# Five reorderings in a gated attention kernel: where a projection's products stand, when row factors are spread, which PSUM banks are used at the end, how wide a mask is, and which load goes first

## The chip, the core and the metric

The kernel runs on one core of a Trainium2 chip. The metric is the device time of the whole program in microseconds (us), as the median of repeated runs. One further run was taken with the hardware profiler. Its page and its trace are what is read below. TensorE is written PE in the profile, its weight loads PEld, VectorE is DVE, ScalarE is ACT, GpSimd is POOL, and SyncE, which issues nearly all transfers, is SP.

## The reference

Two attention blocks A and B of 32 heads with 16 channels run on the same x (2048 rows, 512 columns), and a gate mixes them. A is causal attention inside four chunks of 512 rows, mixed with a linear-attention memory that is carried from chunk to chunk. B is full attention over all 2048 rows.

```
g = sigmoid((x * gate_w).sum(-1))
A, for each of 4 chunks of 512 rows:
    p     = softmax(q k^T / 4 + causal mask);  a_dot = p v
    a_mem = (phi(q) M) / (phi(q) z + 1e-6)           # memory of the earlier chunks
    o     = sig(beta) * a_mem + (1 - sig(beta)) * a_dot
    M += phi(k)^T v ;  z += sum(phi(k))
B:  p = softmax(q k^T / 4) over all 2048 rows ;  o = p v
out = g * (oA @ woA) + (1 - g) * (oB @ woB)
```

## The kernel before, in words

The order of every engine's work is written out by hand: an instruction stands in its engine's queue where the Python code calls it, and engines wait for each other only through semaphores that follow from the data.

**First stage (about 0 to 353 us).** x is loaded in 16 tiles of 128 rows (`load_x`), turned on PE (`do_x`), and split into a high and a low part. Queries, keys and values of A and B are projected (`qk_job`, `v_job`: twelve products of 512 columns each, for high and low parts) and stored to DRAM. `dot_gate` on DVE multiplies x with `gw`, which `load_gate` has spread over the partitions. For A, blocks `blk` 0 to 15 stand for four head groups g by four chunks c. In block 1, 5, 9 and 13 `mem_upd(g, 0)` makes the first memory out of turned keys and the values that `load_vm(g, 0)` brought. SP issues in its own order: at the last value tile it loads B's first keys (`load_kb(0)`) and queries (`load_q(32)`), and only at block 0 the memory's values (`load_vm(0, 0)`).

**Pairs (about 353 to 1975 us).** A loop over k from 0 to 31 works on one unit of B and one of A at a time; a unit is four heads by 512 queries. I call one turn of it a pair. It has 37 groups n: 32 for B (two for each of 16 key tiles) and 5 for A. A group is:

- `t_group` (L502): keys times queries into two PSUM banks, then two exponentials on ACT (L508, 128x512 each), and for A a causal select on POOL (L511);
- one task that finds row maxima for the unit after it: `s_b` (L448, two products into a two-bank tile `SBK`, and a DVE reduction of 1024 columns, L450), or `s_a` for A (L427, with the causal mask added by small products, L430, reduced in L434 and L436);
- `pv` (L524): probabilities times values into the bank `PVB`, one key tile behind. Group 1 of a pair has no `pv`.

`m_chain` (four short DVE instructions, L459 to L469, after group 21) and `m_rows` (PE L475, ACT L477, four transfers L483, at group 24) turn the maxima into rows that are appended to the queries. Exponentials of B and A take their banks from a rotation of three, `T3` (TB0, TB1, MB), the one used longest ago first.

**Factors and projection.** Each unit's result goes to DRAM and back (`fin_copy`, `fin_load`); `fin_rec` makes a row factor on DVE; `fin_bc` (SP, L560) spreads it into the tile `d`; `fin_norm` on POOL multiplies (L564), and for later chunks adds (L569), every second pair. POOL takes its work in order but does not wait for the pair's groups, so a `fin_norm` starts when its factor has landed. From pair 8 on, every even pair ends with `out_split` (ACT L583, POOL L584), and `out_mm` does the twelve products of one half of the output projection in each pair from 9 on (L590), before group 20's `pv`; the first half's sum is copied by ACT (L594), the second's added by DVE (L597).

**Last pair and end.** In pair 31 no maxima are left to find, so the two banks of `SBK[0]` join the rotation: five banks. After it the last four row tiles are projected (`tail_mm`, L617) into the four banks of `SBK[1]` and `SBK[0]`, `TAIL`, and copied out in halves by DVE (L628) and ACT (L626).

The mask of `s_a` is two products a block and row half, both 128 columns wide: the first covers query rows 0 to 63 of the block, the second rows 64 to 127. In the second the first 65 columns of the mask are zero, since those keys are not ahead of any such query.

Of the kernel before, what the change touches and what calls it, by code (L numbers as in the profile page):

```python
# [26 lines left out]
EARLY = 6  # L27
S_FIRST = 10
S_LAST = 10
OMI = 10  # L30


@with_exitstack
def gated_mix_kernel(ctx, tc, x, wq, wk, wv, wo, beta, wqkv, wob, gate_w, out):
    nc = tc.nc
# [381 lines left out]
    def s_a(u, i, p):  # L417
        mx = pair_max(chain_of(u))
        n = 128 * (i + 1)
        b = rot("s", SBK)  # L420
        todo_p = [(0, p)] if p is not None else [(0, 0), (256, 1)]
        for c0, p in todo_p:
            for n2 in range(3):
                for j in (1, 0):
                    r = slice(64 * j, 64 * j + 64)
                    if n2 == 0:
                        nc.tensor.matmul(b[:, j, c0:c0 + n], q_of(u)[r, p, i * 128:(i + 1) * 128], k_of(u, p)[r, :n],  # L427
                                         start=True, stop=False)
                    else:
                        nc.tensor.matmul(b[:, j, c0 + n - 128:c0 + n], crows[r, n2 - 1], cmask[r, n2 - 1],  # L430
                                         start=False, stop=n2 == 2)
        m = mx[:, 0].rearrange("q (j p) i -> q j p i", j=2)
        if len(todo_p) == 1:
            nc.vector.tensor_reduce(m[:, :, p, i], b[:, :, :n], axis=AX.X, op=OP.max)  # L434
        else:
            nc.vector.tensor_reduce(m[:, :, :, i], b.rearrange("q j (p k) -> q j p k", p=2)[:, :, :, :n], axis=AX.X,  # L436
                                    op=OP.max)
# [204 lines left out]
        load_x(tt)  # L642
    identity()
    load_w("B", 0)
    load_gate()
    for tt in range(4, 8):
        load_x(tt)
    constants()

    for tt in range(3):  # L650
# [34 lines left out]
    for tt in range(NT):  # L685
        v_job("A", tt)
        if tt == 2:
            split_w(0, "A", 0)
            do_gate()
        if tt == 3:  # L690
            load_beta()
        if tt in (7, 9, 11):
            load_wv("B", (tt - 7) // 2)
        if tt == NT - 1:
            load_kb(0)
            load_q(32)
        if ax:
            set_aux(*ax.pop(0))
# [21 lines left out]
    for blk in range(16):  # L720
        g, c = divmod(blk, 4)
        pg, pc = divmod(blk - 1, 4)
        if blk == 4:
            mode["misc"] = TB + [MB, PVB]
        if 4 <= blk < 14:
            quota += len(ST_A + ST_B) / 10
        if blk == 14:
            for p in range(2):
                set_aux(KB[1][:, p], 0, nc.sync)
            load_kb(1, 0)  # L730
        if blk == 0:
            load_vm(0, 0)
        n = blk + 1 + (c == 2)
        if c < 3 and n < 16:
            load_vm(n // 4, n % 4)
        qk_job(0, "A", g, 0, c)
        if c == 3 and g < 3:
            split_w(0, "A", g + 1, (0,))
        spill()
        if blk == 0:  # L740
            split_wv(3)
            do_beta()
        if blk > 0:
            if pc == 0:
                mem_upd(pg, pc)
        qk_job(0, "A", g, 1, c)
        spill()
        if c == 2 and g < 3:
            load_w("A", g + 1)
        if c == 3 and g < 3:  # L750
            split_w(0, "A", g + 1, (1,))
        if blk == 4:
            load_q(33)
            load_ka(0)
            load_q(0)
            load_va(0)
        if blk == 6:
            load_w("B", 1)
        for f, n in ((store_gate, 5), (load_grow, 7), (do_grow, 10)):
            if blk == n:  # L760
                f()
        if blk == 14:
            m_chain(0)
        if blk == 15:
            m_rows(0)
        want = CUM[blk]
        mt = [[], [], []]
        if c > 0:
            mt[0] += [todo(mem_out, g, c)]
            mt[2] += [todo(mem_put, g, c)]  # L770
        if c < NC4 - 1:
            mt[1 + (c == 0)] += [todo(mem_tr, g, c)]
        for n in range(3):
            for f in mt[n]:
                f()
            if blk == 14 and n == 2:
                quota = EARLY
            if mt[n]:
                spill()
            if blk == 14:  # L780
                load_kb(1, 1 + n)
            if nf == 35:
                mode["misc"] = [MB, PVB, TB[1]]
            if nf < want:
                fill[nf]()
                spill()
                if nf in (18, 24):
                    load_w("B", 2 + nf // 24)
                if nf in (15, 20, 26):
                    split_w(2 if nf == 20 else 1, "B", nf // 5 - 2)  # L790
                nf += 1
        if blk == 13:
            for f in first:
                f()
            first, quota = [], 0
        if 0 < c < NC4 - 1:
            mem_upd(g, c)
        if blk == 14:
            spill()
        if blk == 15:  # L800
            for f in early:
                f()
        if nf >= 16 and "vb" not in AT:
            AT["vb"] = 1
            load_vb(0)
# [13 lines left out]
            set_aux(KB[2][:, p], 0)  # L819

    T3 = TB + [MB]
    TAIL = [b[:, n] for b in SBK[::-1] for n in range(2)]
    mode["misc"] = T3
    NG = 2 * NT + 5

# [22 lines left out]
    def extras(k):  # L848

        pre, post = {}, {}  # L850
        if not k:
            for n in range(4):
                pre[2 * n] = [fill[n - 4]]
        post[2 * S_LAST + 4] = [todo(m_rows, k + 1)]
        for n, it in [(k - 9, OMI)] + [(23, 14)] * (k == 31):
            if n >= 0:
                pre[2 * it] = [todo(out_mm, n // 8, n // 2 % 4, n % 2)]
        return pre, post

    def beside(k, it):  # L860

        for f, it0, u in ((fin_load, NT + 1, 32 + k), (fin_rec, 5, 31 + k), (fin_bc, 6, 31 + k),
                          (fin_load, 1, k - 1), (fin_rec, 6, k - 1), (fin_bc, 7, k - 1)):
            if it == it0 and (k or it0 > NT):
                f(u)
        c, j = divmod(k - 1, 8)
        if k and j % 2:
            for kd, it0 in (("B", 9), ("A", 13)):
                if it == it0:
                    fin_norm(kd, j // 2, c)  # L870
        if k >= 8 and k % 2 == 0 and it == NT + 2:
            out_split(k // 8 - 1, k // 2 % 4)
        if (k, it) == (31, 4):
            grest = AT["grest"] = AT["o"][0][64:, 0, 0]
            nc.sync.dma_start(grest, GD[3 * C:].rearrange("(o t) -> o t", o=1).to_broadcast([64, C]))
        if (k, it) == (31, 9):
            grest = AT["grest"]
            nc.vector.tensor_scalar(grest, grest, nh[64:, 3:4], None, op0=OP.mult)
        if (k, it) == (31, NT + 2):
            fin_rec(63)  # L880
        if k == 31 and it == 13:
            o = AT["o"][1][:64, 3, 0]
            nc.gpsimd.tensor_tensor(o, o, AT["d"][0][:64], op=OP.mult)
        if k == 31 and it < 8 and it % 2 == 0:
            for a in range(2):
                tail_split(it // 2, slice(0, 3), a)
# [17 lines left out]

    for k in range(32):
        ua, ub = k, 32 + k
        banks = T3 + [SBK[0][:, n] for n in range(2)] * (k == 31)
        for n in range(NG):
            it = n // 2 if n < NG - 1 else NT + 2
            t_group(*(ub, n) if n < 2 * NT else (ua, n - 2 * NT), banks)  # L910
            for f in plan.get((k, n), []) + ex[k][0].get(n, []):
                f()
            pvs(k, n)
            for f in ex[k][1].get(n, []):
                f()
            if n % 2 == 0 and n < NG - 1:
                continue
            beside(k, it)
            if it == S_LAST:
                m_chain(k + 1)  # L920
            if it == 4 and not k:
                late()
            if it == 4 and not k:
                load_q(ub + 2)
                for c in range(NC4):
                    load_kb(2, c)
            if it == NT and k < 29:
                load_q(ub + 3)
                load_kb(k + 3)
            if it == 6 and k < 31:  # L930
                load_q(ua + 1)
                load_ka(ua + 1)
                if (ua + 1) % 2 == 0:
                    load_va(ua + 1)
            if it == 9:
                if k % 2 == 0 and k < 30:
                    load_vb(k // 2 + 1)
                if 1 <= k <= 4:
                    load_wo(k - 1)
# [55 lines left out]
```

## Time and profile before

| | |
|---|---|
| median of the runs shown | 2007.81 us (2006.12 to 2014.9) |
| the profiled execution | 2007.75 us; its span 2006.0 us, 1.75 us around it |
| busy: PE, DVE, ACT, POOL | 1956.3, 1631.9, 1435.1, 256.6 us |
| chain that ended last | PE 89%, DMA 3%, DVE 3%, ACT 2%, SP's queue 2% |
| pairs 0 to 31 | start at 352.6 us; pair 9 starts at 801.7, pair 31 at 1924.7, the end begins at 1974.8 |

All times on the trace's axis count from the span's start. A row of the timeline gives start, length, engine, line, operation, tiles (out<-in) and count of merged instructions; in brackets stands the idle time of the engine before it and what ended that. A row of the stretches gives its length, each engine's busy time with its count, and PEclk, the share of full clock that PE was granted. PE's ends are modelled, so starts are the better clock.

### The profile page before, as it was taken

How to read it: one execution, taken by the hardware profiler on the slowest of the kernel's cores; microseconds unless marked ns; L12 is line 12 of the kernel's file. 1: busy time of each engine (PE TensorE's matmuls, PEld its weight loads, DVE VectorE, ACT ScalarE, POOL GpSimd, SP SyncE). 2: the span in 40 equal slices, each digit the busy share in tenths (PEclk: the TensorE clock that was granted, in tenths of full speed). 3: DMA queues.
4: the chain of work that ended last, by engine and by line, in shares of the span. 5: the costliest groups of instructions: out<-in, count | busy, mean ns of one | idle time of the engine just before them, and what ended most of it. 6: DMA issues, size and time to landing. Idle time of an engine off the chain costs nothing.

```text
span 2006.0 us, 43688 instructions
## 1 busy us (share of the span) xinstructions
PE 1956.3 (98%) x17517; PEld 949.0 (47%) x17517; DVE 1631.9 (81%) x1825; ACT 1435.1 (72%) x2703; POOL 256.6 (13%) x474
## 2 busy tenths in 40 slices
PE   8999999999999999999999999999999999999988
PEld 7777777444444344444444444444444444444434
DVE  6135665799999999999999999999899999899832
ACT  3233332688888888888787888787878787878883
POOL 2200000011110101111111111111111111111111
PEclk9999999999999999999999999999999999999999
DMA  7765656644443445343435344444444545444101
GB/s 222 164 190 177 197 180 177 148 106 112 95 112 85 104 93 109 81 110 81 109 79 112 85 112 85 112 85 112 85 112 85 112 85 111 85 112 85 50 26 54
DMA packets 162743, 222.49 MB, mean 111 GB/s; under 512 B 39261, under 2 KB 89453, under 8 KB 156781
## 3 DMA queue, kind: packets, MB, share of 16 engines
q1 hardware_dynamic: 159596, 211.70, 43.9%
q0 software_dynamic: 2944, 8.00, 2.2%
q8 instruction: 138, 2.26, 0.5%
q14 instruction: 65, 0.52, 0.1%
HBM read 148.21 MB, written 68.16 MB: 108 GB/s over the span
## 4 chain that ended last, share of the span: by engine, by line
PE 89%; DMA 3%; DVE 3%; ACT 2%; SPq 2%; issue 1%; POOL 0%; ACTq 0%; POOLq 0%; DVEq 0%
PE pvb L524 31%; PE tb L502 17%; PE sbk L448 12%; PE mb L502 8%; PE tb L279 3%; PE sbk L427 2%; PE tb L590 2%; PE mb L279 2%; ACT raw L508 2%; PE pvb L279 2%; DVE mxb L450 2%; PE sbk L430 2%; PE mb L590 1%; PE sbk L279 1%; PE tb L262 1%
## 5 line engine op out<-in xcount | busy, mean ns | idle before, releaser
L450 DVE TENSOR_REDUCE mxb<-sbk 128x2 f32<-128x1024 f32 x1024 | 1222.7, 1222 | 49.4 <-PE sbk L448 45.7
L508 ACT ACTIVATE raw<-tb 128x512 f32<-128x512 f32 x1557 | 886.0, 596 | 172.8 <-PE tb L502 85.6
L524 PE MATMUL pvb<-raw,vb 128*17 128x256 f32 (+1 forms) x8072 | 639.5, 389 | 0.0
L508 ACT ACTIVATE raw<-mb 128x512 f32<-128x512 f32 x780 | 465.2, 596 | 81.6 <-PE tb L502 57.5
L502 PE MATMUL tb<-qb,xh 64*128 64x512 f32 x880 | 330.9, 494 | 3.7 <-ACT raw L508 3.7
L524 PEld LDWEIGHTS pvb<-raw,vb 128*17 128x17 f32 x8072 | 133.8, 95 | 344.8 <-issue 338.4
L448 PE MATMUL sbk<-xh,qb 64*128 64x512 f32 x1344 | 287.6, 400 | 4.4 <-DVE mxb L450 3.3
L511 POOL TENSOR_SCALAR_AFFINE_SELECT raw<-raw 128x256 f32<-128x256 f32 (+1 forms) x320 | 115.4, 361 | 879.9 <-ACT raw L508 871.9
L502 PE MATMUL mb<-qb,xh 64*128 64x512 f32 x437 | 215.6, 493 | 2.0 <-ACT raw L508 2.0
L502 PEld LDWEIGHTS tb<-qb,xh 64*128 64x128 f32 x880 | 124.7, 183 | 190.5 <-issue 98.3
L502 PE MATMUL tb<-qb,kb 64*128 64x512 f32 x463 | 176.0, 496 | 4.8 <-ACT raw L508 2.8
L434 DVE TENSOR_REDUCE mx<-sbk 128x2 f32<-128x768 f32 (+1 forms) x128 | 139.8, 1092 | 43.9 <-PE sbk L430 36.2
L448 PE MATMUL sbk<-kb,qb 64*128 64x512 f32 x704 | 152.9, 408 | 0.8 <-DVE mxb L450 0.7
L448 PEld LDWEIGHTS sbk<-xh,qb 64*128 64x128 f32 x1344 | 138.8, 186 | 10.8 <-DVE mxb L450 7.0
L502 PEld LDWEIGHTS mb<-qb,xh 64*128 64x128 f32 x437 | 79.9, 183 | 89.5 <-issue 49.1
L502 PE MATMUL mb<-qb,kb 64*128 64x512 f32 x241 | 118.4, 491 | 0.8 <-DVE st L289 0.8
L502 PEld LDWEIGHTS tb<-qb,kb 64*128 64x128 f32 x463 | 65.8, 183 | 102.3 <-issue 51.4
L524 PE MATMUL pvb<-raw,va 128*17 128x256 f32 (+2 forms) x1280 | 94.7, 383 | 4.2 <-ACT pvs L533 0.8
L564 POOL TENSOR_TENSOR o<-o,d 128x512 f32<-128x512 f32 x31 | 39.7, 1282 | 415.2 <-DMA qa<-dA 177.0
L427 PE MATMUL sbk<-ka,qa 64*128 64x256 f32 (+3 forms) x512 | 86.6, 346 | 0.0
L502 PE MATMUL tb<-qa,ka 64*128 64x384 f32 (+3 forms) x340 | 79.5, 372 | 0.0
L448 PEld LDWEIGHTS sbk<-kb,qb 64*128 64x128 f32 x704 | 72.1, 185 | 12.6 <-issue 6.5
(265 smaller groups left out, 1804.5 us busy)
## 6 DMA issues: line engine op xcount, KB each, us to landing
xh<-dB SPq DMA_DIRECT2D x38, 512.0 KB
vb<-vdB SPq DMA_DIRECT2D x16, 1088.0 KB
dB<-st SPq DMA_DIRECT2D x64, 256.0 KB
dA<-st SPq DMA_DIRECT2D x64, 256.0 KB
pd<-pvs SPq DMA_DIRECT2D x64, 256.0 KB
kb<-dB SPq DMA_DIRECT2D x22, 512.0 KB
xh<-dB SPq DMA_DIRECT2D x38, 256.0 KB
qb<-dB SPq DMA_DIRECT2D x64, 128.0 KB
```

What stands on the lines that cost most here:

```text
L279: nc.tensor.matmul(b, WS[ws][w][wi][:, k, :], (XH, XL)[xi][c][:, k, :], start=n == 0, stop=n == 11)
L427: nc.tensor.matmul(b[:, j, c0:c0 + n], q_of(u)[r, p, i * 128:(i + 1) * 128], k_of(u, p)[r, :n], start=True, stop=False)
L430: nc.tensor.matmul(b[:, j, c0 + n - 128:c0 + n], crows[r, n2 - 1], cmask[r, n2 - 1], start=False, stop=n2 == 2)
L434: nc.vector.tensor_reduce(m[:, :, p, i], b[:, :, :n], axis=AX.X, op=OP.max)
L448: nc.tensor.matmul(b[:, j], q_of(u)[r, p, i * 128:(i + 1) * 128], k_of(u, p)[r, kc * C:(kc + 1) * C], start=True, stop=True)
L450: nc.vector.tensor_reduce(MXB[u][:, :, p, i, kc], b, axis=AX.X, op=OP.max)
L502: nc.tensor.matmul(bs[j][:, c0:c0 + w], k_of(u, h // 2)[r, 128 * it:128 * it + 128], q_of(u)[r, h // 2, q0:], start=True, stop=True)
L508: nc.scalar.activation(pt, bs[j], AF.Exp, scale=SCALE)
L511: nc.gpsimd.affine_select(out=m, in_=m, pattern=[[1, 128]] if n < 2 else [[0, 2], [1, 128]], compare_op=OP.is_ge, fill=0.0, base=0, channe ...
L524: nc.tensor.matmul(PVB[32 * h:32 * h + E + 1, q0 + lo:q0 + hi], vt[:, it, 4 * q + h, :], pt[:, lo:hi], start=it == 0 and lo == 0, stop=it ...
L564: nc.gpsimd.tensor_tensor(o, o, d, op=OP.mult)
L590: nc.tensor.matmul(b, (AT["oh"], AT["ol"])[oi][:, g, a], (AT["wh"], AT["wl"])[wi][:, g, a], start=n == 0, stop=n == 11)
```

## The change

- `extras`: the twelve products of `out_mm` move from group 20 (`OMI` = 10, two groups an iteration) to group 1 of each pair from 9 on. `OMI` = 14 now places only the one extra half in pair 31, at group 28, where it was.
- `beside`: `fin_bc` for A's unit k-1 moves from iteration 7 to iteration 12 (`S_LAST` + 2), so in SP's queue it passes the loads of iteration 9 (`vb`, and `om` into `d`), and the transfers of `m_rows`.
- In pair 31 the rotation takes the first bank of each `SBK` tile in place of both banks of `SBK[0]`; `TAIL` becomes TB0, TB1, MB and the first bank of `SBK[0]`.
- `s_a`: the second mask product covers the last 64 columns in place of 128.
- `load_vm(0, 0)` moves from block 0 to the last value tile, ahead of `load_kb(0)` and `load_q(32)`.
- `load_gate` moves behind x's tiles 4 to 7.

```diff
-OMI = 10
+OMI = 14
...
-                        nc.tensor.matmul(b[:, j, c0 + n - 128:c0 + n], crows[r, n2 - 1], cmask[r, n2 - 1],
+                        w = 192 - 64 * n2
+                        nc.tensor.matmul(b[:, j, c0 + n - w:c0 + n], crows[r, n2 - 1], cmask[r, n2 - 1, 128 - w:],
                                          start=False, stop=n2 == 2)
...
     load_w("B", 0)
-    load_gate()
     for tt in range(4, 8):
         load_x(tt)
+    load_gate()
...
         if tt == NT - 1:
+            load_vm(0, 0)
             load_kb(0)
             load_q(32)
...
-        if blk == 0:
-            load_vm(0, 0)
...
-    TAIL = [b[:, n] for b in SBK[::-1] for n in range(2)]
+    TAIL = T3 + [SBK[0][:, 0]]
...
-        for n, it in [(k - 9, OMI)] + [(23, 14)] * (k == 31):
+        for n, at in [(k - 9, 1)] + [(23, 2 * OMI)] * (k == 31):
             if n >= 0:
-                pre[2 * it] = [todo(out_mm, n // 8, n // 2 % 4, n % 2)]
+                pre[at] = [todo(out_mm, n // 8, n // 2 % 4, n % 2)]
...
-                          (fin_load, 1, k - 1), (fin_rec, 6, k - 1), (fin_bc, 7, k - 1)):
+                          (fin_load, 1, k - 1), (fin_rec, 6, k - 1), (fin_bc, S_LAST + 2, k - 1)):
...
-        banks = T3 + [SBK[0][:, n] for n in range(2)] * (k == 31)
+        banks = T3 + [b[:, 0] for b in SBK] * (k == 31)
```

## The prediction

> **What bounds the kernel now.** I read the chain of waits first (PE 89%, in the table above), then the span in 40 slices, then stretches cut at each pair's first exponential, then the timeline where stretches differ.
>
> ```profile
> PE   8999999999999999999999999999999999999988
> ...
> 609.00:657.00 48.00, 47.61 (x500) 19.31 (x494) 45.95 (x48) 40.67 (x77) 3.61 (x10) 1.00 0.41 91
> 657.00:705.70 48.70, 47.60 (x500) 19.15 (x494) 46.74 (x48) 40.72 (x76) 6.17 (x12) 1.00 0.47 103
> 801.70:852.60 50.90, 50.51 (x510) 21.47 (x508) 45.93 (x48) 41.26 (x77) 5.93 (x11) 1.00 0.38 82
> 1669.30:1721.90 52.60, 50.88 (x512) 21.52 (x508) 48.13 (x49) 41.59 (x78) 7.59 (x14) 1.00 0.52 109
> 1924.70:1974.80 50.10, 41.14 (x280) 14.97 (x276) 11.27 (x28) 38.34 (x75) 5.72 (x9) 0.97 0.09 30
> ...
> 801.70:1875.30 1073.60, 1062.43 (x10591) 450.76 (x10588) 975.43 (x998) 869.96 (x1617) 140.28 (x251) 1.00 0.44 95
> ```
>
> The first row is PE's busy share by slice. In the others the length and the busy time of PE, PEld, DVE, ACT and POOL stand behind the stretch; they are pairs 5, 6, 9, 26 and 31, then pairs 9 to 29 together. The reader is to see three things. PE fills a pair (47.61 of 48.00 us), so what PE no longer does or waits for comes off the time; DVE is close behind with 45.95. A pair with twelve products is 2.90 us longer (50.90 against 48.00). Some pairs with the same PE work are longer still (pair 6 by 0.70, pair 26 by 1.70), with DVE busier by 0.8 and 2.2. Pair 31 is another case: no engine is full.
>
> **The change, part by part.** *The memory's values ahead of the keys.*
>
> ```profile
> 104.09 2.15 PE L350 MATMUL sbk<-vm,pk 128*128 128x136 f32 x8 [3.34 <-DMA vm<-vdA]
> ...
> 105.88 3.78 PE L279 MATMUL sbk<-xh,ws 128*128 128x512 f32 x8
> ...
> 104.00:110.70 6.70, 6.61 (x21) 5.68 (x22) 0.30 (x1) 0.00 (x0) 0.00 (x0) 0.55 0.77 258
> ...
> 165.45 1.19 PE L350 MATMUL mb<-vm,pk 128*128 128x136 f32 x8
> ...
> 166.39 2.12 PE L279 MATMUL pvb<-xh,ws 128*128 128x512 f32 x8
> ```
>
> PE stands 3.34 us until the values land, and then runs at a granted clock of 0.55: the eight memory products take 2.15 where they later take 1.19, the next eight 3.78 where others take 2.12. With the load ahead of eight key and query transfers, wait and slow clock both go: 3.34 + 0.96 + 1.66 = 6.0 us. PE is full in the slices that follow (nines above), so they stay gone. Late next are keys and queries, which the first maxima need in block 4 only. Range: 3.3 (the clock drops anyway) to 6.3.
>
> *The projection's products.* Now at group 20, for 2.90 us. The place where they go, then the place where they stand (pair 9):
>
> ```profile
> 801.66 2.37 POOL L584 TENSOR_TENSOR ol<-o,oh 128x1024 fp32r<-128x1024 f32 x1 [0.55 <-ACT oh L583]
> ...
> 802.61 0.50 PE L502 MATMUL tb<-qb,kb 64*128 64x512 f32 x2
> 802.95 0.40 PE L448 MATMUL sbk<-xh,qb 64*128 64x512 f32 x2
> ...
> 804.51 0.63 PE L524 MATMUL pvb<-raw,vb 128*17 128x256 f32 x8
> 805.07 0.49 PE L502 MATMUL tb<-qb,kb 64*128 64x512 f32 x1
> ...
> 826.30 0.57 PE L448 MATMUL sbk<-xh,qb 64*128 64x512 f32 x2
> ...
> 826.80 1.19 PE L590 MATMUL tb<-wh,oh 128*128 128x512 f32 x4
> ...
> 829.75 0.63 PE L524 MATMUL pvb<-raw,vb 128*17 128x256 f32 x8
> ```
>
> Groups 1 and 2 take 802.61 to 805.07, 2.46 us. Two groups of the mean (48.00/37 = 1.30) take 2.59 with two `pv`; these hold one less (804.51 to 805.07, 0.56). So about half a microsecond is a wait: group 2 needs banks that group 1's exponentials still read, and PE has nothing in between. Twelve products there give them time. Step by step from start to start: group 1's scores 0.34, maxima to first product 0.50 (826.30 to 826.80), products 2.95 (826.80 to 829.75), then group 2's scores 0.34, maxima 0.33 (I take the first figure for it), `pv` 0.56: 5.02. That is 2.56 more than 2.46, so 0.34 less than today, times 22 pairs (9 to 30): 7.5 us. Range 0 (the wait reappears behind the products, since ACT's copy of the sum now stands ahead of group 2's exponentials) to 0.56 x 22 = 12.3. The low part `ol` lands at 804.03; PE wants it at the ninth product, about 803.45 + 8 x 0.245 = 805.4, so it doesn't wait.
>
> *A's factors later.* Pair 26, with the undisturbed instruction of pair 16 (1190.22) behind it, and pair 16's transfers:
>
> ```profile
> 1699.48 1.28 POOL L564 TENSOR_TENSOR o<-o,d 128x512 f32<-128x512 f32 x1 [4.97 <-DMA d<-rd]
> ...
> 1700.04 0.76 DVE L467 TENSOR_SCALAR mhi<-mx 128x32 fp32r<-128x32 f32 x1
> ...
> 1703.39 0.50 PE L448 MATMUL sbk<-xh,qb 64*128 64x512 f32 x2 [1.34 <-DVE mxb L450]
> ...
> 1190.22 0.18 DVE L467 TENSOR_SCALAR mhi<-mx 128x32 fp32r<-128x32 f32 x1
> ...
> 1182.08 0.53 SPq L560 DMA_DIRECT2D d<-rd  x1
> ...
> 1187.23 1.27 POOL L564 TENSOR_TENSOR o<-o,d 128x512 f32<-128x512 f32 x1 [5.04 <-DMA d<-rd]
> ...
> 1194.76 1.03 SPq L483 DMA_DIRECT2D qa<-mr  x2
> ...
> 1203.20 0.29 POOL L511 TENSOR_SCALAR_AFFINE_SELECT raw<-raw 128x128 f32<-128x128 f32 x1 [13.34 <-ACT raw L508]
> ```
>
> While POOL multiplies, DVE's short instruction of `m_chain` lasts 0.76 us, not 0.18, reductions queue behind it, and PE waits 1.34. Whether the two meet depends on when the factor lands. Pairs 9 to 29 took 1073.6 us where 21 x 50.90 is 1068.9; with pair 6 that is 4.7 + 0.7, of which I take 4.5, as two other pairs were long by 0.3 with nothing met. Spread behind `m_rows`, the factor is issued after the chain, so A's multiply can no longer meet it: 4.5 us (0 to 5.4). B's multiply ended 4.97 us before A's began (POOL's idle time), 5.5 us ahead of the chain, and moves at most 2.6 us later with the products. What it costs: the issue comes at 1194.76 + 1.03 = 1195.8; by the 5.15 us of today (1182.08 to 1187.23) POOL starts at 1200.9 and ends its two instructions at 1203.6, when the first select is due (1203.20). Its result is read two groups later, so I charge nothing.
>
> *The mask.*
>
> ```profile
> L430 PE MATMUL sbk<-cmask,crows 64*128 64x128 bf16 x1024 | 74.2, 221 | 0.0
> ...
> L430 PEld LDWEIGHTS <-crows 64*128 64x128 bf16 x1024 | 31.8, 95 | 22.8 <-issue 9.0
> ```
>
> 1024 products are 256 blocks of two by two row halves, and the halves overlap. Half of the columns of the second go. At the pace of the products above (2.95/12 = 0.246 us for 512 columns) 64 columns are 31 ns, times 256: 7.9 us as upper end; nothing, if the weight loads (95 ns each, unchanged) set the pace. I take 5, nearer the upper end, since the column count sets the pace in every longer product here. [...]
>
> *Pair 31's banks.*
>
> ```profile
> PEld sbk L502 <- ACT raw L508: 15.6, 12, 2.3
> ...
> 1940.47 0.70 ACT L508 ACTIVATE raw<-sbk 128x512 f32<-128x512 f32 x1
> ...
> 1941.22 0.50 PE L502 MATMUL sbk<-qb,xh 64*128 64x512 f32 x1 [1.46 <-ACT raw L508]
> ...
> 1924.18 0.50 PE L502 MATMUL sbk<-qb,xh 64*128 64x512 f32 x2 [0.34 <-DVE mx L436]
> ```
>
> PE's write into one bank of `SBK[0]` starts 0.05 us after ACT has read the other (1940.47 + 0.70). So a tile is waited for as a whole, and five banks act as four. With the banks in two tiles those waits go. They are 15.6 us, but ACT is busy 38.34 of the pair's 50.10, so at most 11.8 can go before ACT is full, and the products' two halves (2 x 2.90) lie in that. I take 7.4, nearer 11.8 - 5.8 = 6.0 than 11.8. Against it: the last `s_a`, right behind group 0, uses the tile that group 0 now takes as well, and waits for its second exponential: 0.50 + 2 x 0.70 at most behind 1924.18 where 0.34 was enough, of which I take 1.4. Net 6 (0 to 10).
>
> *The end's banks.*
>
> ```profile
> 1996.01 0.38 ACT L626 ACTIVATE raw<-sbk 128x256 f32<-128x256 f32 x1
> 1996.44 0.50 PE L617 MATMUL sbk<-wh,kb 128*128 128x512 f32 x1 [1.06 <-ACT raw L626]
> ...
> 2000.50 0.50 PE L617 MATMUL sbk<-wh,xh 128*128 128x512 f32 x1 [0.99 <-ACT raw L626]
> ```
>
> The same, with nothing to hide it: 1.06 + 0.99 and a slow first step after each, 2.3 us (2.0 to 2.5).
>
> *The gate's load.* It lands later by up to four x tiles.
>
> ```profile
> GB/s 222 164 190 177 197 180 177 148 106 112 95 112 85 104 93 109 81 110 81 109 79 112 85 112 85 112 85 112 85 112 85 112 85 111 85 112 85 50 26 54
> ...
> 18.75 0.68 DVE L172 TENSOR_TENSOR xl<-mb,xh 128x512 fp32r<-128x512 f32 x1
> ...
> 21.90 1.09 PE L279 MATMUL sbk<-xl,ws 128*128 128x512 f32 x4
> ```
>
> DVE's gate products then start late and push the low parts of x, ready at 19.43 and used at 21.90: 2.47 us of cover. Four tiles are 1 MB, 4.7 us at the first slice's 222 GB/s. Cost 0, at most 4.7 - 2.5 = 2.2, if DVE had no idle time to absorb any of it.
>
> Sum: 6.0 + 7.5 + 4.5 + 5 + 6 + 2.3 = 31.3 us off the profiled 2007.75, which is the median (2007.81) within 0.1: **1976 us**.
>
> **Rivals.** *DVE takes over.* With 45.95 of 48.00 us busy DVE may hold what PE gives: against it, it needs no more than before, and the products give it 2.6 us a pair. If the mask and half the products' gain are lost: 1976 + 5 + 3.7 = 1985. *The pairs of banks are not the cause.* [...] If the waits at 1941.22 and 1996.44 have another cause, the last two parts fall to nothing: 1976 + 8.3 = 1984. The 0.05 us behind the other bank's reader speaks against it: that wait is the program's. *The values' wait moves.* If another transfer stops PE at 104 instead: 1982. *Slower.* The factor lands too late. POOL's two multiplies then stand ahead of A's selects, `pv` of A waits for these, and PE with it, in 11 even pairs (10 to 30). PE is held where landing takes over some 7.6 us (5.15 now, and 2 to 3 us till the select is read); the whole gain is gone from 7.6 + 31/11 = 10.4 us on; at 12 us it is 4.4 us each, 48 in all: 1976 + 48 = 2024. Fewer transfers are around it there (at 1182 keys and queries were), which speaks against it. *All upper ends* but pair 31's: 1976 - 4.8 - 2.9 - 1 = 1967.
>
> **Chances.** Forecast 0.62, DVE 0.12, banks 0.06, values 0.08, upper ends 0.09, slower 0.03. The range 1966 to 1990 holds these but the slow case, with some room above for two at once. A change of 0.5%, 10 us, is about what a measurement of this kernel can tell from none. Faster by more than that (under 1998): 0.93; within: 0.04; slower: 0.03.
>
> **What would show it.** Values: no wait at L350 near 100 us, clock 1.0 from 85 to 117. Products: group 1 to group 3 of pair 9 in 5.0 us, pairs 9 to 29 at about 50.4, all alike; L467 never over 0.2. Mask: pair 5 at 47.8. Pair 31: `sbk` waits for ACT under 3 us, pair under 45. End: L617 without a gap, 29 us from 1974.8's counterpart. The prediction is wrong if pairs 9 to 29 stay near 50.9, or if POOL's selects wait for L569.

## The result, and the profile after

The changed kernel takes 1979.96 us (median of 6 runs, 1974.66 to 1984.97) against 2008.95 us for the kernel before (6 runs beside it, 2006.12 to 2015.15). The ratio is 0.985, 95% interval 0.983 to 0.987. The profiled execution took 1977.74 us (span 1976.0) against 2007.75 (span 2006.0), so 30.0 us less. In the rows, lines from L430 on are numbered one higher than before.

The two spans, cut at the first exponential of the pairs and at the first product of the end (L617 before, L618 after):

| stretch | before | after | difference |
|---|---|---|---|
| first stage and pair 0 | 417.05 | 412.80 | -4.2 |
| pairs 1 to 8 | 384.68 | 385.19 | +0.5 |
| pairs 9 to 29 | 1073.61 | 1057.07 | -16.5 |
| pair 30 | 49.38 | 48.72 | -0.7 |
| pair 31, to the end's first product | 52.26 | 45.70 | -6.6 |
| end | 29.05 | 26.53 | -2.5 |

Two rows lean on these two executions. Ten profiles of kernels that are alike up to there (this one and nine of the experiments below) have pair 1 begin between 412.8 and 420.5 us, at 415.9 in the mean; the one of the changed kernel here is the earliest, and of the kernel before there is one profile only. In pair 31 the kernel before ran 3.4 us at half of the full clock (0.50 in the row that follows), the changed kernel at 1.00; what that is worth is read with the banks, below.

```profile
1929.40:1932.80 3.40, 3.40 (x16) 0.65 (x12) 3.26 (x10) 2.43 (x6) 0.00 (x0) 0.50 0.28 80
```

Next the stretches of the changed kernel (length, busy time of PE, PEld, DVE, ACT and POOL with counts, PEclk, DMA share, GB/s): pairs 5, 6, 9 and 26, pair 31, the end, then pairs 9 to 29 together.

```profile
606.00:653.90 47.90, 47.46 (x498) 19.30 (x494) 45.92 (x48) 40.68 (x77) 3.63 (x10) 1.00 0.40 90
653.90:701.80 47.90, 47.46 (x498) 19.29 (x494) 45.91 (x48) 40.66 (x77) 6.20 (x12) 1.00 0.47 106
798.00:848.30 50.30, 50.14 (x512) 21.31 (x506) 46.04 (x48) 41.28 (x77) 5.94 (x11) 1.00 0.37 84
1653.90:1704.10 50.20, 50.04 (x510) 21.22 (x506) 46.67 (x49) 41.70 (x77) 7.53 (x14) 1.00 0.51 113
1903.80:1949.50 45.70, 43.72 (x303) 17.23 (x303) 10.98 (x28) 38.11 (x77) 7.07 (x12) 1.00 0.10 34
1949.50:1976.00 26.50, 22.65 (x99) 17.93 (x96) 10.25 (x26) 3.24 (x9) 5.30 (x9) 1.00 0.25 80
798.00:1855.10 1057.10, 1053.74 (x10592) 447.76 (x10586) 973.84 (x998) 871.22 (x1618) 140.79 (x251) 1.00 0.44 97
```

Pairs 6 and 26, long before by 0.70 and 1.70, are now like their neighbours. From pair 9 on PE is busy 50.14 of 50.30 us, with only 0.16 idle where it had 0.39. A pair with twelve products is 2.4 us longer than one without (50.30 against 47.90); before it was 2.9.

The next view is the timeline of PE at the memory products, where PE stood 3.34 us before.

```profile
102.91 1.09 PE L350 MATMUL sbk<-vm,pk 128*128 128x136 f32 x8
103.74 2.11 PE L279 MATMUL sbk<-xh,ws 128*128 128x512 f32 x8
```

The L350 row has no bracket, so PE did not wait, and both groups take what they take elsewhere (1.09 and 2.11, against 1.19 and 2.12 at 165 us before the change; 2.15 and 3.78 at this place before). The clock was 1.00 there (102.9 to 106.6). Now pair 9's groups 1 to 3:

```profile
798.85 0.50 PE L503 MATMUL tb<-qb,kb 64*128 64x512 f32 x2
799.19 0.40 PE L449 MATMUL sbk<-xh,qb 64*128 64x512 f32 x2
...
799.52 1.20 PE L591 MATMUL mb<-wh,oh 128*128 128x512 f32 x4
...
803.68 0.50 PE L503 MATMUL mb<-qb,kb 64*128 64x512 f32 x1
```

From group 1 to group 3 it is 4.83 us, 2.37 more than the 2.46 before, and each step follows the last one without a gap.

One stretch got worse, the start. The rows are 20 to 40 us of the kernel before and of the changed one, then the changed kernel's DVE and SP, SP before, and the arrival of PE at A's first keys, before and after.

```profile
20.00:40.00 20.00, 20.00 (x104) 16.76 (x104) 17.91 (x42) 9.59 (x18) 0.22 (x1) 1.00 0.60 198
20.00:40.00 20.00, 17.37 (x85) 14.13 (x84) 14.91 (x34) 7.21 (x15) 0.00 (x0) 0.91 0.60 189
...
14.44 0.69 DVE L179 SCALAR_TENSOR_TENSOR scr<-raw,gw 128x512 bf16<-128x512 f32 x1 [2.82 <-DMA gw<-in_gate_w_dram]
15.22 2.51 SPq L161 DMA_DIRECT2D raw<-in_A_x_dram  x4
...
13.08 1.04 SPq L161 DMA_DIRECT2D raw<-in_A_x_dram  x2
...
86.25 2.02 PE L279 MATMUL sbk<-xh,ws 128*128 128x512 f32 x8
88.58 2.02 PE L279 MATMUL sbk<-xh,ws 128*128 128x512 f32 x8
```

PE was full before and now stands for 2.6 us, with a mean clock of 0.91, and reaches A's keys 2.3 us later. DVE waited 2.82 us for the gate's row. Its gate products are the last readers of the buffers of x tiles 0 to 3, so SP could issue tiles 8 to 11 only at 15.22; before, at 13.08.

### The profile page after: what moved, and what is told of

The parts are those of the page before. It is cut to its first block, busy times and chain, and to the rows that moved or that the text cites. A ratio compares the mean times of both kernels' runs of the same rounds, so it can differ in the third digit from the quotient of the medians.

```text
span 1976.0 us, 43643 instructions
## 1 busy us (share of the span) xinstructions
PE 1944.8 (98%) x17517; PEld 945.6 (48%) x17517; DVE 1630.3 (83%) x1825; ACT 1435.7 (73%) x2703; POOL 257.5 (13%) x474
## 4 chain that ended last, share of the span: by engine, by line
PE 90%; DMA 3%; DVE 2%; ACT 2%; issue 1%; SPq 1%; ACTq 0%; DVEq 0%
PE pvb L525 31%; PE tb L503 17%; PE sbk L449 12%; PE mb L503 8%; PE tb L279 3%; PE tb L591 2%; PE mb L279 2%; PE sbk L427 2%; PE pvb L279 2%; PE tb L262 2%; DVE mxb L451 1%; ACT raw L509 1%; PE mb L591 1%; PE mb L262 1%; PE sbk L431 1%
## 5 line engine op out<-in xcount | busy, mean ns | idle before, releaser
L449 PE MATMUL sbk<-xh,qb 64*128 64x512 f32 x1344 | 283.1, 398 | 2.0 <-DMA xh<-dB 0.8
L503 PE MATMUL mb<-qb,xh 64*128 64x512 f32 x445 | 219.6, 494 | 0.0
L427 PE MATMUL sbk<-ka,qa 64*128 64x256 f32 (+3 forms) x512 | 86.8, 346 | 1.2 <-ACT raw L509 1.2
```

The source lines that it names most:

```text
L449: nc.tensor.matmul(b[:, j], q_of(u)[r, p, i * 128:(i + 1) * 128], k_of(u, p)[r, kc * C:(kc + 1) * C], start=True, stop=True)
L503: nc.tensor.matmul(bs[j][:, c0:c0 + w], k_of(u, h // 2)[r, 128 * it:128 * it + 128], q_of(u)[r, h // 2, q0:], start=True, stop=True)
```

## The experiments

Each kernel is the changed one with one edit, if nothing else is said, and its profile is read stretch by stretch. That matters: the first stage differs by several us between executions of the same code. In the kernel with the products at group 12, whose code is the same up to pair 8, pair 0 begins at 357.5, in the changed kernel at 349.9. So spans alone decide nothing of 2 or 3 us. Behind the first stage pairs 9 to 29 repeat well (1056.9 to 1057.4 us in the eight profiles that share the changed kernel's pairs 1 to 29), and so does the end (26.4 to 26.5). Pairs 1 to 8 do not (384.1 to 386.4 in nine profiles), and pair 31 takes either 45.7 or about 47.3.

**The gate's row first.**

```diff
+    load_gate()
     for tt in range(4, 8):
         load_x(tt)
-    load_gate()
```

> The changed kernel, but the gate's row is loaded ahead of x tiles 4 to 7 again. Theory: the late row is what cost the start of the changed kernel 2.4 us. VectorE waited 2.82 us for it at 14.44, its gate products release the buffers of x tiles 8 to 11, so these tiles were loaded 2.1 us later and TensorE stood for 2.6 us between 20 and 40 us. With the row first again TensorE is busy without a gap from 20 to 40 (20.0 of 20.0 us), the first product of A's keys (L279 behind L262, 88.58 in the changed kernel) comes at about 86.2, and the span falls by 2.4. Rival: the tiles themselves now queue behind each other and the row has nothing to do with it; then the gap between 20 and 40 stays and the span stays within 0.5.

PE from 20 to 40 us here, and in the kernel with four repairs below, which has the row first too:

```profile
20.00:40.00 20.00, 19.56 (x101) 16.03 (x100) 17.21 (x39) 9.53 (x18) 0.17 (x1) 1.00 0.60 190
20.00:40.00 20.00, 20.00 (x105) 16.79 (x104) 17.91 (x42) 9.60 (x18) 0.00 (x0) 1.00 0.60 196
```

The stretch went as the theory says: the three kernels with the row first, that of before included, have PE busy 19.56 to 20.00 us there, the eleven with the row late 16.44 to 18.97. A's first keys come at 86.08 here. The span did not: 1979.0, 3.0 more than the profiled changed kernel. Pairs 3 and 8 were longer (386.4 for pairs 1 to 8; both vary between executions of this code, as is told below), a wait near 128 us took 2.0 back, and pair 31 took 47.3. The row's cost is shown for its stretch, at 2.5 us for this pair of executions (88.58 against 86.08). The eleven profiles with the row late reach A's first keys between 86.8 and 92.7 us, at 89.5 in the mean, the three with the row first between 86.1 and 87.0. For the whole the cost is under what one profile can tell.

**The memory's values behind the keys again.**

```diff
         if tt == NT - 1:
-            load_vm(0, 0)
             load_kb(0)
...
+        if blk == 0:
+            load_vm(0, 0)
```

> The changed kernel, but the memory's first values are loaded behind the keys and queries again. Theory: TensorE waits for them again near 103 us for about 3.3 us, the granted clock falls to about 0.55 behind that wait, and the next eight products take 3.8 us instead of 2.1; the span rises by 6.0 to 6.4. Rival, the clock falls whatever the wait (the slow stretch belongs to this place): the span rises by 3.3 only, since the products were slow before too. Rival, the wait was taken over by another: no more than 1 us.

```profile
108.53 2.15 PE L350 MATMUL sbk<-vm,pk 128*128 128x136 f32 x8 [3.83 <-DMA vm<-vdA]
110.32 3.73 PE L279 MATMUL sbk<-xh,ws 128*128 128x512 f32 x8
...
108.40:115.00 6.60, 6.47 (x22) 5.55 (x23) 0.30 (x1) 0.00 (x0) 0.00 (x0) 0.59 0.77 257
```

Wait and slow clock (0.59) are back together: 3.83, and 2.15 + 3.73 where the changed kernel has 1.09 + 2.11, so 3.83 + 2.68 = 6.5 us. The slow clock stands behind the wait in both executions that have it (0.55 and 0.59) and not in the changed kernel at the same products (1.00), so by these three it goes with the wait, not with the place. The span rose by 8.8; the rest lies in the first stage ahead of this place, which varies.

**The products away from the wait.**

```diff
-        for n, at in [(k - 9, 1)] + ...
+        for n, at in [(k - 9, 12)] + ...
```

> The changed kernel, but the projection's twelve products stand ahead of group 12 instead of group 1, far from the chain and from POOL's multiplies. Theory: group 1 gains because TensorE has a wait of half a microsecond there for the banks of group 0; elsewhere the products cost their full 2.9 us. So pairs 9 to 29 without a collision take 50.8 to 50.9 us each instead of 50.29, and the stretch of 21 pairs grows by 11 to 12. Rival, leaving group 20 (beside the chain and POOL's multiplies) is what gained: the pairs stay at 50.3 and the stretch within 2 us. By the prediction's own sum (0.34 a pair) it grows by 7.

Pair 9, and pairs 9 to 29:

```profile
805.30:856.10 50.80, 50.36 (x510) 21.40 (x506) 46.10 (x48) 41.30 (x77) 5.89 (x11) 1.00 0.38 83
805.30:1873.80 1068.50, 1059.11 (x10591) 451.26 (x10586) 976.63 (x998) 871.06 (x1618) 140.53 (x251) 1.00 0.42 96
```

The stretch grows by 11.4 us, 0.54 a pair. What gained is group 1, not the leaving of group 20.

**A's factor at step 7 again.**

```diff
-(fin_bc, S_LAST + 2, k - 1)
+(fin_bc, 7, k - 1)
```

> The changed kernel, but A's factor is spread at step 7 of the pair again, as before the change. Theory: A's multiply on POOL meets the chain's short instructions on VectorE again in a few pairs: L467 lasts up to 0.8 to 1.3 us in these instead of 0.18, pairs 9 to 29 grow by about 4.7 us in all, pair 6 by 0.7, while the pairs that meet nothing stay at 50.29; pairs 1 and 3, which are 1.2 and 0.4 us long in the changed kernel, return to 47.9. Rival, moving the products already took the meetings away: pairs 9 to 29 grow by less than 1 us.

Pairs 9 to 29, then POOL, DVE and PE in pair 12, the longest with 53.5 us:

```profile
797.70:1865.60 1067.90, 1055.59 (x10590) 447.17 (x10586) 983.69 (x998) 872.85 (x1617) 140.72 (x251) 1.00 0.44 96
...
979.38 1.28 POOL L565 TENSOR_TENSOR o<-o,d 128x512 f32<-128x512 f32 x1 [5.22 <-DMA d<-rd]
979.54 1.16 DVE L468 TENSOR_SCALAR mhi<-mx 128x32 fp32r<-128x32 f32 x1
...
983.29 0.49 PE L449 MATMUL sbk<-xh,qb 64*128 64x512 f32 x2 [1.70 <-DVE mxb L451]
```

The short DVE instruction ends when POOL's ends (980.66 and 980.70), and PE waits 1.70 us behind the chain. The mechanism is the predicted one. The size is not: the stretch grew by 10.9 us, not 4.7, and eight of the ten even pairs of this stretch from 10 to 28 meet. An estimated 1.7 of it is the clock: its mean over pair 12 is 0.97 of 53.5 us, as 3.4 us at 0.50 would give, and two products behind the wait (984.62) lasted 0.79 us where they lasted 0.50 at 981.05. The rest is timing: with the products in group 1 A's reciprocal, and the factor with it, comes 2.4 us later in a pair, and the chain 0.6 earlier. A's multiply starts 29.5 to 31.4 us into the even pairs here and 27.0 to 30.2 in the kernel before; L468 is due at 30.1 to 30.4 here, L467 at 30.7 to 31.0 before. Pair 6, expected 0.7 longer, took 47.9, since the factor landed behind the chain there. Pairs 1 and 3 took 47.9 and 48.0, as expected, but the changed kernel comes near that in other executions too (see the next experiment). Not every DVE instruction was held: in pair 1 of the changed kernel a reduction from 442.44 on took 1.21 us (the mean of all 1024 is 1.22) beside a POOL subtraction that began at 442.47 and took 1.26.

**The weights behind the chain.**

```diff
-            if it == 9:
-                if k % 2 == 0 and k < 30: load_vb(k // 2 + 1)
-                if 1 <= k <= 4: load_wo(k - 1)
+            if it == 9 and k % 2 == 0 and k < 30: load_vb(k // 2 + 1)
+            if it == 12 and 1 <= k <= 4: load_wo(k - 1)
```

> The changed kernel, but the projection's weights are loaded and split at step 12 instead of step 9 of pairs 1 to 4, behind the chain of step 10. Theory: with A's factor no longer ahead of them, POOL's copies and subtractions of the weights now run beside the chain in pairs 1 and 3 and hold VectorE's short instructions (L467 1.31 and 0.51 us instead of 0.18). Moved behind the chain they do not meet it: pairs 1 and 3 take 47.9 like pairs 2, 4 and 5, and the span falls by 1.5. Rival, the long pairs have another cause: they stay at 49.1 and 48.3. It may also go wrong: POOL's work then stands ahead of A's selects, and pairs 1 to 4 grow.

Pair 1 of the changed kernel, then pairs 1 and 2 of this one; POOL and DVE in pair 1 of the changed kernel; POOL in pair 2 of this one, and its first select in pair 2 of the changed kernel:

```profile
412.80:461.90 49.10, 47.54 (x500) 19.25 (x494) 47.15 (x48) 40.74 (x76) 7.34 (x14) 1.00 0.42 95
...
415.30:463.30 48.00, 47.55 (x501) 19.41 (x496) 46.01 (x48) 40.80 (x77) 7.16 (x14) 1.00 0.47 100
463.30:512.40 49.10, 48.18 (x498) 19.58 (x494) 45.91 (x48) 40.73 (x77) 9.57 (x16) 1.00 0.55 118
...
440.55 1.28 POOL L578 TENSOR_TENSOR wl<-o,wh 128x512 fp32r<-128x512 f32 x1
440.56 1.31 DVE L468 TENSOR_SCALAR mhi<-mx 128x32 fp32r<-128x32 f32 x1
...
505.43 1.27 POOL L565 TENSOR_TENSOR o<-o,d 128x512 f32<-128x512 f32 x1
506.66 1.40 POOL L512 TENSOR_SCALAR_AFFINE_SELECT raw<-raw 128x128 f32<-128x128 f32 x5
...
502.62 0.30 POOL L512 TENSOR_SCALAR_AFFINE_SELECT raw<-raw 128x128 f32<-128x128 f32 x1 [2.54 <-ACT raw L509]
```

Pairs 1 and 3 take 47.9, as the theory says. By itself that shows little, since the changed kernel's own second profile has 47.95 and 48.10 there: it matters when the weights land. In nine profiles with the weights at step 9 and the late factor, pair 1 or 3 is long (48.3 to 49.1) in the eight cases where POOL's first subtraction starts less than 28.3 us into the pair, and takes 47.9 to 48.1 in the ten where it starts later. In the rows above it starts at 27.7 (440.55 - 412.8). With the weights at step 12, here and in two kernels below, no pair 1 or 3 is over 48.0. Pairs 2 and 4 break in the way it names at the end: weights and A's multiply stand ahead of the selects. The first select starts 43.4 us into the pair (506.66 - 463.3) in place of 40.7 (502.62 - 461.9), 2.7 us late, and the pair is 1.2 longer. That is the mechanism of the prediction's slower rival, started by other work, with a price: of 2.7 us of lateness some 1.5 are covered, where the prediction had 2 to 3.

**Pair 31 with both banks of one tile, and with seven banks.**

```diff
-        banks = T3 + [b[:, 0] for b in SBK] * (k == 31)
+        banks = T3 + [SBK[0][:, n] for n in range(2)] * (k == 31)      # first kernel
+        banks = T3 + [b[:, n] for n in range(2) for b in SBK] * (k == 31)   # second kernel
```

> The changed kernel, but the scores of pair 31 use both banks of the first two-bank tile again instead of one bank of each tile. Theory: a tile of two banks is waited for as a whole, so five banks act as four. The waits of L503 on sbk for ACT come back (23.7 us in all before the change, under 2 in the changed kernel), and the time from the pair's first exponential to the first product of the end rises from 45.7 to about 52, by 6.6. Rival, what gained there was the place of the out products and of the narrower mask: it rises by less than 2.

> The changed kernel, but the scores of pair 31 use all four banks of the two tiles beside the three single ones, seven instead of five. Theory, the tile is waited for as a whole: the second bank of a tile brings no freedom and gives a new wait, so the stretch from the first exponential to the first product of the end is not shorter than 45.7 and probably longer, 47 to 52. Rival, each bank is waited for by itself: two banks more give TensorE more room and the stretch is 44 to 45.7.

Weight loads and waits in pair 31 of the changed kernel (up to 1946), then stretch and waits of the kernel with one tile, and of the one with seven banks:

```profile
L503 PEld LDWEIGHTS sbk<-qb,xh 64*128 64x128 f32 x25 | 3.6, 183 | 5.2 <-issue 4.3 <-ACT raw L509 0.8
...
1907.60:1958.50 50.90, 42.55 (x304) 15.82 (x298) 11.42 (x28) 39.28 (x77) 7.13 (x12) 1.00 0.09 30
PEld sbk L503 <- ACT raw L509: 14.6, 12, 1.8
...
1903.90:1959.60 55.70, 48.03 (x302) 18.53 (x303) 10.98 (x28) 39.66 (x77) 7.02 (x12) 0.94 0.09 28
PEld sbk L503 <- ACT raw L509: 14.6, 18, 1.4
```

With one tile the waits return (0.8 to 14.6 us) and the stretch is 5.2 longer, not the 6.6 of the change. The clock fits the difference of 1.4: this execution had 1.00 through the pair, where the kernel before ran 3.4 us at 0.50, which costs an estimated 1.7 at most (half of 3.4). So 5.2 is what the banks gave by this run, and the rest of the 6.6 most likely came with the clock, by chance. Two banks more do not help: the waits are the same 14.6, in 18 places in place of 12, and the stretch is 10.0 longer, more than the 47 to 52 that was expected. An estimated 3.3 of that is a low clock (0.94 of 55.7 us). A bank whose neighbour in the tile was being read was not free: 14.6 us of waits in both kernels, 0.8 with the banks in different tiles. Different banks are read and written in all three; what differs is the tile, which by these waits the program guards as a whole.

**Group 0 of pair 31 on the single banks.**

```diff
-            t_group(..., banks)
+            t_group(..., banks if n else T3)
```

> The changed kernel, but group 0 of pair 31 uses the three single banks only. Theory: in the changed kernel the last scores of A's maxima behind group 0 wait for the exponential that reads the other bank of their tile (1.2 us on ACT's side; group 1 starts 2.89 us after group 0, before the change 1.47). Without that tile in group 0 the two groups are 1.5 us apart again and pair 31 is 1.4 us shorter. Rival: ACT is full in this pair, so what is gained at its start is waited for later: under 0.5 us.

The wait at the start of pair 31 in the changed kernel, and the whole pair here:

```profile
1904.92 0.33 PE L427 MATMUL sbk<-ka,qa 64*128 64x128 f32 x2 [1.17 <-ACT raw L509]
...
1906.50:1950.90 44.40, 43.58 (x300) 17.06 (x296) 11.75 (x28) 38.08 (x78) 7.26 (x12) 1.00 0.11 35
```

1.3 us shorter, and pair 30 before it by 0.4 (48.31). It is worth more in some executions. Seven profiles have the changed kernel's pair 31 with this wait of 1.17 us: it took 45.7 to 45.8 in three and 47.2 to 47.3 in four. The three kernels with group 0 on single banks took 44.4 to 44.5. In the kernel with the gate's row first the same wait was followed by products at a clock of 0.63, and pair 31 took 47.3. The three rows are the wait there, the products, and the same products in the changed kernel:

```profile
1904.70:1907.90 3.20, 2.01 (x24) 1.03 (x24) 0.72 (x2) 1.38 (x3) 2.34 (x1) 1.00 0.14 37
1907.90:1912.50 4.60, 4.60 (x14) 3.32 (x12) 4.46 (x10) 1.09 (x2) 0.00 (x0) 0.63 0.23 66
1906.50:1909.40 2.90, 2.90 (x14) 2.17 (x12) 2.80 (x7) 1.09 (x2) 0.00 (x0) 1.00 0.23 90
```

**The end in the two-bank tiles again.**

```diff
-    TAIL = T3 + [SBK[0][:, 0]]
+    TAIL = [b[:, n] for b in SBK[::-1] for n in range(2)]
```

> The changed kernel, but the four output sums of the end stand in the two two-bank tiles again. Theory: the first product behind a copy of the other bank waits for it (1.06 and 0.99 us before the change), and the end takes 29.0 us instead of 26.5, by 2.5. Rival, the gain came from pair 31's end and not from the banks: 26.5 stays.

```profile
1955.60:1984.70 29.10, 23.22 (x99) 17.80 (x96) 10.24 (x26) 3.28 (x9) 5.27 (x9) 1.00 0.22 73
1975.16 0.50 PE L618 MATMUL sbk<-wh,kb 128*128 128x512 f32 x1 [1.06 <-ACT raw L627]
1979.21 0.50 PE L618 MATMUL sbk<-wh,xh 128*128 128x512 f32 x1 [0.99 <-ACT raw L627]
```

2.6 us, with the same two waits as before the change.

**Four repairs together**, timed on one chip beside the same without the gate's row, and the changed kernel itself.

```diff
+    load_gate()                                  # ahead of x tiles 4 to 7 (first kernel only)
...
-            if it == 9: load_wo
+            if it == (12 if k % 2 else 9): load_wo
...
-(fin_rec, 6, k - 1)
+(fin_rec, 8, k - 1)
...
-            t_group(..., banks)
+            t_group(..., banks if n else T3)
```

> The changed kernel with four repairs: the gate's row ahead of x tiles 4 to 7; the projection's weights at step 12 in the odd pairs 1 and 3, and still at step 9 in the even ones; the reciprocal for A's factor at step 8 instead of 6; group 0 of pair 31 on the single banks. Theory: each stretch gains by itself, as read from the runs before: the start 2.4 us at TensorE's 87 us mark, pairs 1 and 3 together 1.5, pair 8 up to 1.3 (VectorE waits there for the factor's denominators, 1.30 us before the reciprocal), pair 31 1.3 to 2.9 (with the clock that falls there in some runs). In all 5 to 8 us under the changed kernel on the same chip, 0.3 to 0.4%. Rival: the start's DMA landings vary by several us from run to run and drown the rest; then the median differs by less than 2.

> As the kernel with the four repairs, but the gate's row stays behind x tiles 4 to 7. Theory: 3 to 6 us under the changed kernel, and 2.4 above the one with the row first. Rival, the row does not matter: the two are alike within 1.

> The changed kernel itself, as the measure for the two kernels beside it on the same chip, and a second look at what varies: by the runs so far the time at which TensorE reaches A's first keys lies between 86 and 93 us, pair 8 is long by 0 to 1.6 us, and pair 31 takes 45.7 or 47.3. The pairs 9 to 29 should take 1057 again within 1 us.

| kernel | median of 4 runs | range | ratio to before, 95% interval |
|---|---|---|---|
| four repairs | 1976.94 us | 1974.69 to 1981.24 | 0.9835 (0.9818 to 0.9852) |
| three, row late | 1980.72 us | 1977.42 to 1981.37 | 0.9852 (0.9836 to 0.9869) |
| changed kernel | 1982.30 us | 1980.23 to 1983.14 | 0.9858 (0.9843 to 0.9872) |

Pair 8, pair 31, and pairs 9 to 29 with the four repairs:

```profile
749.40:797.30 47.90, 47.46 (x498) 19.26 (x494) 46.11 (x48) 41.61 (x78) 6.26 (x13) 1.00 0.49 107
1903.60:1948.10 44.50, 43.68 (x301) 17.12 (x297) 11.76 (x28) 38.11 (x78) 7.30 (x12) 1.00 0.11 35
797.30:1855.20 1057.90, 1054.45 (x10590) 448.01 (x10586) 978.24 (x998) 871.34 (x1617) 140.77 (x251) 1.00 0.45 97
```

The medians stand in the expected order, 5.4 and 1.6 us under the changed kernel (5 to 8 and 3 to 6 were expected), but the intervals of the ratios overlap: that the whole is faster than the changed kernel is likely and not shown. What is shown are stretches. Pairs 1, 3 and 8 take 47.9 to 48.0, pair 31 44.5. Pair 8 took 47.9 to 49.5 us in the ten profiles with the late factor and the reciprocal at step 6, and 48.1 and 48.0 in the two with the factor at step 7; in one of the ten DVE is seen to wait 1.30 us for the transfer with the factor's denominators, and why that lands late was not tried. Something is given back. Pairs 9 to 29 take 0.9 us more, and pair 2 takes 48.3 and 48.6 in the two profiles in place of 47.9; the reciprocal now stands nearer to the chain, which was not tried by itself. The changed kernel's second profile repeats pairs 9 to 29 (1057.0) and pair 31 (45.7), but its pair 1 begins 6.6 us later than in the first. With the row first the profiled execution took 1974.6 us of span.

## Why the prediction was right, and where its terms were off

Forecast 31.3 us off, measured 30.0 in the profiled executions and 29.0 in the medians. The mechanisms held, but for the gate's load; that the total came so near is partly luck: the products gave 4.4 us more than their term, while the mask, A's factor and the gate's load fell short by about 6 together, and chance helped in the profiles (1.4 of clock in pair 31, an early first stage).

- *Values ahead of keys, 6.0.* By the rows at the place 3.34 + (2.15 - 1.09) + (3.78 - 2.11) = 6.1, and 6.5 by undoing it. Right in size and mechanism at the place, though the first stage's variation hides most of it: pair 1 begins only 1.1 us earlier in the mean of the ten profiles than in the one of the kernel before.
- *The gate's load, 0 (at most 2.2).* Cost 2.3 here, 2.5 against the kernel with the row first. The step that failed is the cover: I counted the low parts that queue behind the gate products on DVE, and not the buffers that those products release. What was late next was a DMA on SP, x tiles 8 to 11.
- *The products, 7.5, or 0.34 a pair.* Measured 0.54 a pair, 11.9 in 22 pairs. The step is "maxima to first product 0.50": that was read in group 20, where it is 0.50, but in group 1 it is 0.33 (799.19 to 799.52). The rest of the chain of starts held: 4.83 us by rows against 5.02. The range had it (to 12.3).
- *A's factor, 4.5.* Pairs 9 to 29 lost 16.5 us, of which 21 clean pairs account for 21 x 0.62 = 13.0 (50.91 to 50.29), so 3.5 are meetings, and pair 6 adds 0.7. But the weights' work on POOL, behind the factor in SP's order until now, moved into the chain of pairs 1 and 3: 1.5 back, net 2.7. Other executions put this price between 0 and 1.9, and pair 8 adds to it: pairs 1 to 8 take 385.1 us in the mean of nine profiles with the late factor and 383.7 in the one with it at step 7. I had asked what waits behind the moved transfer, not what comes earlier since it no longer stands in front. Alone the term is misleading: with the products in group 1 the late factor saves 10.9 in pairs 9 to 29, of which an estimated 1.7 was the clock.
- *The mask, 5.* Measured 0.1 a pair (48.00 to 47.90 in pair 5), near 3 in all; no run undoes the mask by itself. The narrow product got 27 ns shorter:

```profile
L430 PE MATMUL sbk<-cmask,crows x1024: 216/222/230, 289.3 to 1924.9; 64*128 64x128 bf16 x171
L431 PE MATMUL sbk<-cmask,crows x1024: 189/208/230, 285.8 to 1905.4; 64*128 64x128 bf16 x96, 64*128 64x64 bf16 x75
```

  These are shortest, median and longest. Before all were 128 columns wide, after half of them are 64 wide, and these are the shortest: 216 became 189 (the median of 208 lies between the two widths). At 256 of them that would be 6.9 us, so fewer than half of these gains reach the pair's end. The upper end was taken for the likely value; where the rest stays was not tried.
- *Pair 31, 6.* 6.6 in the table, 5.2 by undoing it. The prediction's row showed the clock at 0.97 and the sum gave it no term; that is most likely the rest. The start conflict that I set against it, 1.4, was 1.3.
- *The end, 2.3.* 2.5.

Of the rivals none came about. DVE did not take over (its share of a pair is about the same, 0.90 and 0.92, and PE idles less), the banks were the cause, the values' wait did not move. The slower one, selects behind A's multiply, did not happen in the changed kernel: A's second instruction in pair 26 ends before the first select.

```profile
1695.29 1.28 POOL L570 TENSOR_TENSOR o<-o,d 128x512 f32<-128x512 f32 x1
1696.94 0.29 POOL L512 TENSOR_SCALAR_AFFINE_SELECT raw<-raw 128x128 f32<-128x128 f32 x1 [0.37 <-ACT raw L509]
```

The margin is 0.4 us there. The signs named ahead held, with two exceptions: L468 went over 0.2 us in pairs 1 and 3, and pair 5 took 47.9, not 47.8.

## What to carry to other kernels

Put work that waits for nothing into the slot where the full engine waits for a buffer, and price it there, start by start, with that slot's own rows and not those of the slot it leaves. When a transfer moves back in a queue, ask what moves forward, and when a load moves back, ask which buffers its readers would have released. Two banks in one tile counted as one for the waits seen here (14.6 us in pair 31, against 0.8), so a rotation should take its banks from different tiles. Read the clock of a stretch before its gain is put down to a change: 3.4 us at half clock were worth about 1.6 here.

## What was not expected of the hardware

The granted clock fell behind a short stall. In pair 31 PE was busy 2.01 of 3.20 us, then got 0.63 of the clock for the next products in one execution; in another it was busy 2.08 of 3.30 and got 1.00. The wait was 1.17 us in both. Four of seven executions with this wait took the longer 47.2 to 47.3 us. In pair 31 of the kernel before the fall was 3.4 us at 0.50, and the 0.63 over 4.6 us is what 3.4 us at 0.50 would give; with seven banks a mean of 0.57 over 8.0 us (1906 to 1914) fits twice that, an estimated 6.9 us at 0.50. What decides whether the clock falls was not shown. The price was 1.6 us for a stall of 1.2.
